# Reordering the first unit's output accumulation and giving the fourth unit its own step plan in a fused attention and mixer kernel

## The chip, the cores and the metric

The kernel runs on one core of a Trainium2 chip. The metric is the device time of one execution, in microseconds (us), and the median of several runs is compared. The core has a matrix engine (TensorE, "PE" in the profile, with "PEld" for its weight loads), a vector engine (VectorE, "DVE"), a scalar engine (ScalarE, "ACT"), GpSimd ("POOL") and SyncE ("SP"), each with its own instruction stream. Transfers between the chip's memory and the on-chip SBUF are issued here by SyncE and GpSimd (two by ScalarE).

## The reference: what is computed

Inputs: q, k, v of shape (8 batches, 8 heads, 576 rows, 64), and four weights. Keys and values are averaged over groups of eight rows, the queries attend to the 72 pooled keys, and the result, with the heads side by side (576 x 512 per batch), goes through an MLP mixer. Its token part mixes the 576 rows through a width of 256; its channel part mixes the 512 channels through a width of 1536.

```python
k_p, v_p = (t.reshape(B, H, S // 8, 8, D).mean(axis=3) for t in (k, v))
scores = (1.0 / np.sqrt(D)) * np.matmul(q, k_p.transpose(0, 1, 3, 2))
attn = softmax(scores)                        # exp(s - max) / (sum + 1e-9)
x = np.matmul(attn, v_p).transpose(0, 2, 1, 3).reshape(B, S, H * D)
h = np.maximum(x.transpose(0, 2, 1) @ w_tok1, 0.0) @ w_tok2
u = x + h.transpose(0, 2, 1)
out = u + np.maximum(u @ w_ch1, 0.0) @ w_ch2  # float32, (8, 576, 512)
```

## The kernel before

**Two halves.** The work of a batch has an attention and token half (`batch_steps`) and a channel half (`unit_steps`). The channel half of batch n is *unit* n; a ninth unit (n = 8) does the 64 rows that each batch leaves over from its four full chunks of 128 rows. While TensorE works on unit n, the attention and token steps of the next batch or of the one after are slipped in between.

**A unit** (lines 438 to 478). First twelve blocks m: four matmuls with `w_ch1` into a one-bank PSUM buffer `p1` (L445), and a relu on ScalarE into `GT` (L449). Then four output chunks c of 128 rows: twelve matmuls over the rows m of `w_ch2` are accumulated in one `p1` buffer (L468); VectorE adds `u` into `o` (L473), and SyncE stores `o` (L476). The pool `ps_one`, from which `p1` comes, has three buffers, taken in turn; each is free again when its reader is done. `w_ch2` is loaded in three pieces of four rows m by `load_ch2` (L138), at the start of the kernel, behind other loads.

**Steps.** `unit_steps` is a generator that yields after every second matmul, 24 times in the blocks and 24 times in the chunks. `unit(n, at)` looks up each yield's number in a plan `at` and emits what stands there, so the order on every engine is written out by hand. In the plans, `<` means batch n, no mark batch n + 1, `>` batch n + 2; a step `lX4` loads q, k or v of batch n + 4. Tail steps (`u4`, `M4`, `T4`) are only done for batches of odd number. Plans `FIRST`, `SECOND` and `THIRD` serve units 0, 1 and 2, and `LATER` all others.

**The steps that matter here:**

- `K0 K1 V0 V1` (L145 to L151): GpSimd sums groups of eight rows of k and v.
- `Q0` to `Q3` (L246): VectorE transposes the queries block by block from the loaded `qb` to `qD`.
- `kpT` (L194): TensorE transposes the pooled keys.
- `s0 s1 s2` (L258, L263): scores on TensorE and the exponential on ScalarE. `s0` needs Q0 and Q1, `s1` needs Q2 and Q3. They use the two two-bank buffers `p2` of the pool `ps_two`.
- `av0` to `av4` (L297; L309 and L315): eight matmuls into a `p2` buffer, then on VectorE a reciprocal `den` and a multiplication into `x` (the tail, av4, into `xt`).
- `at0 at1` (L343) and `u0` to `u4` (L358, L359): the token mixing. The fifth matmul of `at0` reads `xt`.
- `M0 M2 M` (L377, L384): `u` has to be transposed before it can be an operand of the next unit. From unit 3 on this goes through memory: SyncE writes `u` out (`mem`), and four reads bring it back as `v`, with blocks of 32 rows side by side.
- `T0` to `T4` (L390): VectorE transposes the 32 x 32 blocks of `v` into `uT`.
- `lq4 lk4 lv4` (L103, L86): GpSimd issues the loads of batch n + 4. q, k and v have two buffers each, so a load of q waits until the batch two before it has been read by its Q3.

Of the kernel before, what the change touches and what calls it, by code (L numbers as in the profile page):

```python
# [8 lines left out]
FP32 = mybir.dt.float32  # L9
BF16 = mybir.dt.bfloat16  # L10
AF = mybir.ActivationFunctionType
ALU = mybir.AluOpType
# [8 lines left out]
def kernel(  # L21
# [14 lines left out]
    nc = tc.nc  # L36
    B, H, S, D = q.shape
    P = 128
    POOL = 8
    SP = S // POOL  # L40
    BP, BR = 64, S // 64
# [4 lines left out]
    DM = H * D  # L46
    DT = moe_w_tok1.shape[1]
    DC = moe_w_ch1.shape[1]
    NM = DC // P
# [9 lines left out]
    outp = ctx.enter_context(tc.tile_pool(name="outp", bufs=4))  # L59
    ps_one = ctx.enter_context(tc.tile_pool(name="ps_one", bufs=3, space=bass.MemoryType.PSUM))  # L60
# [8 lines left out]
    w_ch2 = singles.tile([P, NM, DM], BF16)  # L69
# [4 lines left out]
    u_tails = singles.tile([P, 4, DM], BF16)  # L74
# [30 lines left out]
    def q_pairs(a0, a1):  # L105
        return q[0, 2 * a0:2 * a1].rearrange("(a l) (p r) d -> (l p) a (r d)", l=2, r=BR)

    def load(key, b):
        if b < B:
            load_q(b) if key == "q" else load_kv(b, k if key == "k" else v, key)  # L110

    def load_tok():
        nc.gpsimd.dma_start(out=f2, in_=moe_w_tok2.rearrange("(c p) n -> p c n", p=P))
        w = moe_w_tok1.rearrange("(p r) n -> p r n", r=BR)
        for half in range(2):
            rows = slice(half * BP, (half + 1) * BP)
            nc.gpsimd.dma_start(out=w_tok1[rows, 0:4, :],
                                in_=w[:, 0:8, :].rearrange("p (c u) n -> p c u n", u=2)[:, :, half])
        for half in range(2):
            rows = slice(half * BP, (half + 1) * BP)  # L120
            nc.gpsimd.dma_start(out=w_tok1[rows, 4 + half, :], in_=w[:, 8, :])

    def permute_tok2():
        src = f2.rearrange("t m (p r) -> t m r p", r=BR)
        dst = w_tok2.rearrange("t m (r p) -> t m r p", p=BP)
        for m in range(2):
            nc.gpsimd.tensor_copy(out=dst[:, m], in_=src[:, m])
        for half in range(2):
            nc.gpsimd.tensor_copy(out=w_tok2t[:, :, half, half * BP:(half + 1) * BP], in_=w_tok2[:, :, 8 * BP:S])

    def load_ch1():
        for g in range(3):
            cols = slice(g * 512, (g + 1) * 512)
            nc.gpsimd.dma_start(out=w_ch1[:, :, cols], in_=moe_w_ch1[:, cols].rearrange("(p c) n -> p c n", c=4))

    def load_ch2(gs):
        for g in gs:
            nc.gpsimd.dma_start(out=w_ch2[:, 4 * g:4 * g + 4, :],  # L138
                                in_=moe_w_ch2[g * 512:(g + 1) * 512, :].rearrange("(c p) n -> p c n", p=P))
# [298 lines left out]
    def unit_steps(n, st):  # L438

        GT = gtp.tile([P, NM, 4 * P], BF16, name="GT")  # L440
        uT = uT_tails if n == B else st["uT"]
        for m in range(NM):
            ps = ps_one.tile([P, 512], FP32, name="p1")
            for kk in range(4):
                nc.tensor.matmul(out=ps, lhsT=w_ch1[:, kk, m * P:(m + 1) * P], rhs=uT[:, kk, :],  # L445
                                 start=(kk == 0), stop=(kk == 3))
                if kk == 1:
                    yield
            nc.scalar.activation(out=GT[:, m, :], in_=ps, func=AF.Relu)  # L449
            yield  # L450
        for c in range(4):
            if n == B and c == 3:
                for a in range(2):
                    cols = slice(a * 256, (a + 1) * 256)
                    ps = ps_one.tile([P, 512], FP32, name="p1")
                    for m in range(NM):
                        nc.tensor.matmul(out=ps[:, 0:256], lhsT=GT[:, m, c * P:(c + 1) * P], rhs=w_ch2[:, m, cols],  # L457
                                         start=(m == 0), stop=(m == NM - 1))
                    o_sb = outp.tile([P, DM], FP32, name="o")[:, 0:256]
                    nc.vector.tensor_tensor(out=o_sb, in0=ps[:, 0:256], in1=(u_tails if n == B else st["u"])[:, c, cols], op=ALU.add)  # L460
                    for half in range(2):
                        (nc.scalar if half else nc.sync).dma_start(
                            out=out[2 * c + half].rearrange("(p r) n -> p r n", r=BR)[:, 8, cols],
                            in_=o_sb[half * BP:(half + 1) * BP, :])
                continue
            ps = ps_one.tile([P, 512], FP32, name="p1")
            for m in range(NM):
                nc.tensor.matmul(out=ps, lhsT=GT[:, m, c * P:(c + 1) * P], rhs=w_ch2[:, m, :],  # L468
                                 start=(m == 0), stop=(m == NM - 1))
                if m % 2 == 1 and m < NM - 1:  # L470
                    yield
            o_sb = outp.tile([P, DM], FP32, name="o")
            nc.vector.tensor_tensor(out=o_sb, in0=ps, in1=(u_tails if n == B else st["u"])[:, c, :], op=ALU.add)  # L473
            for half in range(2):
                b, r = (2 * c + half, 8) if n == B else (n, 2 * c + half)
                nc.sync.dma_start(out=out[b].rearrange("(p r) n -> p r n", r=BR)[:, r, :],  # L476
                                  in_=o_sb[half * BP:(half + 1) * BP, :])
            yield


    HEAD = """c0 c1 d8 q0 d1 q1 d5 kp0 kp1 kt0 d2 o0 e0 kt1 kp2 kp3 o1 e1 kt2 kt3 q2 q3 d2 o2 e2 vpool0 o3 d1 vpool1 e3 d2
# [8 lines left out]
    THIRD = {0: ">K0 >K1 >V0 >V1 s2", 2: "av0", 4: "av1", 6: "av2", 8: "av3", 10: "av4", 12: "at0 >Q0", 13: "at1",  # L490
             15: "u0", 16: "u1", 18: "u2 t0", 19: "u3", 20: "t1 u4", 22: "t2 >Q1", 24: "t3", 26: "t4", 27: ">Q2 >Q3",
             28: ">kpT lq4 lk4 lv4", 29: ">s0", 33: ">s1", 37: ">s2", 39: ">av0", 41: ">av1", 43: ">av2", 45: ">av3", 47: ">av4"}
    LATER = {0: ">K0 >K1 >V0 >V1 at0", 1: "at1", 3: "u4 M4", 4: "u0", 6: "u1 M0", 7: "u2", 9: "u3 M2 M",
             15: ">Q0", 17: ">Q1", 18: ">kpT", 22: ">s0 >Q2", 24: ">Q3 lq4 lk4 lv4", 27: ">s1", 28: "T0", 30: "T1", 31: "T2",
             33: ">s2 T3", 35: "T4", 37: ">av0", 39: ">av1", 41: ">av2", 43: ">av3", 45: ">av4"}
    warm = singles.tile([P, 512], BF16)

    def head(s):
        if s[0] == "d":
            ps = ps_tr.tile([P, 512], FP32, name="pt")  # L500
            for _ in range(int(s[1:])):
                nc.tensor.matmul(out=ps, lhsT=warm[:, 0:P], rhs=warm, start=True, stop=True)
        elif s[0] == "c":
            a = int(s[1:])
            (nc.vector.tensor_copy if a % 2 else nc.scalar.copy)(out=loaded[0, "q"][:, a, 0:BR * D], in_=qf[:, a, :])
        else:
            batches[0][1][s]()

    def unit(n, at):
        if n + 2 < B:  # L510
            batches[n + 2][0]()
        for i, _ in enumerate(unit_steps(n, batches[n][2] if n < B else None)):
            for s in at.get(i, "").split():
                if s[0] == "l":
                    load(s[1], n + int(s[2]))
                    continue
                ahead = {"<": 0, ">": 2}.get(s[0], 1)
                s = s.lstrip("<>")
                if n + ahead < B and ((n + ahead) % 2 or s not in ("u4", "t4", "M4", "T4")):
                    batches[n + ahead][1][s]()  # L520

    with tc.manual_schedule(engines={PE, POOLE, DVE, ACT, SYNC}):
        batches = [batch_steps(b) for b in range(B)]
        nc.vector.memset(warm, 0.0)
        for a in range(2):
            nc.sync.dma_start(out=qf[:, a:a + 1, :], in_=q_pairs(a, a + 1))
        load("k", 0)
        make_identity(nc, ident)
        load("q", 0)
        load("v", 0)  # L530
        nc.vector.memset(kpz, 0.0)
        nc.vector.memset(w_tok1[:, 4:6, :], 0.0)
        nc.vector.memset(w_tok2t, 0.0)
        load_tok()
        load_ch1()
        load("k", 1)
        permute_tok2()
        load("q", 1)
        load("v", 1)
        load_ch2((0, 1, 2))  # L540
        batches[0][0]()
        for s in HEAD.split():
            head(s)
        load("k", 2)
        load("q", 2)
        batches[1][0]()
        unit(0, FIRST)
        unit(1, SECOND)
        unit(2, THIRD)
        for n in range(3, B + 1):  # L550
            unit(n, LATER)


# [28 lines left out]
```

## Time and profile before

| | |
|---|---|
| time, median of 3 runs | 283.78 us (282.54 to 285.27) |
| the profiled execution | 282.39 us, span on the core 280.6 us |
| granted TensorE clock | 1.00 throughout |
| unit 0: blocks, chunks | 24.5 to 39.7, 39.7 to 58.9 us |
| unit 3: blocks, chunks | 122.8 to 138.2, 138.2 to 152.9 us |
| one 512-column matmul, as the profile lists it | 379 ns |
| output add (L473), block transpose (L390), query transpose (L246) | 683, 680, 776 ns |
| load of q, k or v of one batch | 576 KB |

A line of the timeline gives the start and the length in us, the engine, the line of the code, the operation, what is written and read, how many instructions are merged in it, and in brackets how long the engine had been idle before it and what ended that. A line of the waits gives the waiting engine and line, what it waited for, and the sum in us, the number and the longest. The start of a matmul is measured and its end is modelled, so the distance from start to start is the one to work with.

### The profile page before, as it was taken

To read this page: it belongs to the slowest core of one execution; us is meant where nothing else is said; L and a number is where in the kernel's file an instruction comes from. 1 tells how busy PE (TensorE), PEld (TensorE's weight loads), DVE (VectorE), ACT (ScalarE), POOL (GpSimd) and SP (SyncE) were. 2 spreads that over 40 slices of the span, in tenths; PEclk is the share of its full clock that TensorE was granted. 3 is DMA by queue.
4 is the path that set the end of the run, shared out by engine and by line. 5 is a ranking of instruction groups with operands and counts; after the bars stand their busy time and mean duration, and the time that the engine had idled before them with its cause. 6 is when DMAs were issued, how large, how long until landed. Compare 5 with 4: busy or idle time off the path is not lost.

```text
span 280.6 us, 4530 instructions
## 1 busy us (share of the span) xinstructions
PE 271.3 (97%) x1824; PEld 130.9 (47%) x1824; DVE 141.4 (50%) x272; ACT 111.2 (40%) x187; POOL 130.8 (47%) x121
## 2 busy tenths in 40 slices
PE   8999998999999999999997999999999999999994
PEld 3855444444543545454443444544454444444443
DVE  5466975771575757266239454945484152011012
ACT  2543680039405533614830467046703612602600
POOL 8693311999996991998699995000000000000000
PEclk9999999999999999999999999999999999999999
DMA  8999999970199930892796254315232455015014
GB/s 170 184 204 208 204 201 184 229 163 4 21 163 190 234 51 0 141 222 82 156 176 148 56 136 67 80 39 143 46 77 57 122 84 114 0 37 113 2 42 109
DMA packets 36837, 32.68 MB, mean 116 GB/s; under 512 B 14288, under 2 KB 30288, under 8 KB 36816
## 3 DMA queue, kind: packets, MB, share of 16 engines
q0 software_dynamic: 18672, 17.64, 40.0%
q1 hardware_dynamic: 17984, 14.62, 21.1%
q8 instruction: 14, 0.23, 0.3%
q10 hardware_dynamic: 160, 0.13, 0.2%
q14 instruction: 7, 0.06, 0.1%
HBM read 38.21 MB, written 11.80 MB: 178 GB/s over the span
## 4 chain that ended last, share of the span: by engine, by line
PE 73%; DMA 15%; POOL 4%; DVE 3%; ACT 3%; issue 1%; SPq 0%; DVEq 0%; POOLq 0%
PE p L468 29%; PE p L445 25%; DMA w_ch<-in_moe_w_ch_dram 8%; PE p L358 6%; PE p L343 5%; DMA v<-mem 3%; PE p L297 3%; DMA f<-in_moe_w_tok_dram 3%; PE p L258 2%; ACT ex L263 1%; PE pt L368 1%; POOL vr L86 1%; PE p L457 1%; DVE o L473 1%; ACT GT L449 1%
## 5 line engine op out<-in xcount | busy, mean ns | idle before, releaser
L468 PE MATMUL p<-w_ch,GT 128*128 128x512 bf16 x420 | 101.7, 379 | 1.2 <-DMA w_ch<-in_moe_w_ch_dram 1.2
L445 PE MATMUL p<-uT,w_ch 128*128 128x512 bf16 x384 | 94.5, 379 | 0.1
L449 ACT ACTIVATE GT<-p 128x512 bf16<-128x512 f32 x108 | 64.0, 599 | 75.8 <-PE p L445 75.6
L445 PEld LDWEIGHTS <-w_ch 128*128 128x128 bf16 x432 | 40.3, 97 | 48.1 <-issue 4.4
L468 PEld LDWEIGHTS <-GT 128*128 128x128 bf16 x420 | 38.0, 98 | 43.1 <-issue 4.6
L473 DVE TENSOR_TENSOR o<-p,u 128x512 f32<-128x512 f32 x32 | 21.9, 683 | 32.2 <-PE p L468 32.1
L263 ACT ACTIVATE ex<-p 72x1024 bf16<-72x1024 f32 (+1 forms) x42 | 31.7, 807 | 9.1 <-PE p L258 9.1
L146 POOL TENSOR_TENSOR t<-t 72x512 f32<-72x512 f32 x24 | 30.3, 1262 | 1.9
L145 POOL TENSOR_TENSOR t<-kr 72x1024 f32<-72x1024 bf16 x12 | 25.4, 2120 | 9.6 <-DMA kr<-in_k_dram 8.9
L359 DVE TENSOR_TENSOR u<-p,x 128x512 bf16<-128x512 f32 x32 | 22.1, 691 | 13.9 <-PE p L358 13.7
L145 POOL TENSOR_TENSOR t<-vr 72x1024 f32<-72x1024 bf16 x12 | 25.5, 2121 | 0.9
L390 DVE STREAM_TRANSPOSE uT<-v 128x512 bf16<-128x512 bf16 x16 | 10.4, 686 | 27.1 <-DMA v<-mem 27.1
L334 ACT ACTIVATE AT<-p 128x512 bf16<-128x512 f32 x8 | 4.8, 597 | 46.7 <-PE p L343 43.9
L315 DVE TENSOR_TENSOR x<-p,den 128x512 bf16<-128x512 f32 x30 | 20.7, 692 | 1.0
L297 PEld LDWEIGHTS <-ex 72*128 72x128 bf16 x320 | 15.1, 98 | 12.5 <-DVE x L315 3.4
L246 DVE STREAM_TRANSPOSE qD<-qb 128x576 bf16<-128x576 bf16 x28 | 20.3, 791 | 0.0
L297 PE MATMUL p<-vp,ex 72*128 72x65 bf16 x320 | 16.8, 194 | 2.5 <-DVE x L315 2.1
L358 PE MATMUL p<-AT,w_tok 128*128 128x512 bf16 x64 | 19.0, 379 | 0.0
L309 DVE RECIPROCAL den<-p 128x8 f32<-128x8 f32 (+1 forms) x39 | 7.9, 203 | 16.2 <-PE p L297 15.5
L343 PE MATMUL p<-x,w_tok 128*128 128x512 bf16 x56 | 14.4, 380 | 0.0
L336 DVE TENSOR_SCALAR AT<-p 128x512 bf16<-128x512 f32 x8 | 5.5, 692 | 13.4 <-PE p L343 12.6
L258 PE MATMUL p<-qD,kD 32*72 32x512 bf16 (+1 forms) x224 | 12.2, 295 | 0.1
(90 smaller groups left out, 200.4 us busy)
## 6 DMA issues: line engine op xcount, KB each, us to landing
out_dram<-o SPq DMA_DIRECT2D x70, 128.0 KB, 2.4
kr<-in_k_dram POOLq DMA_DIRECT2D x7, 576.0 KB, 11.1
qb<-in_q_dram POOLq DMA_DIRECT2D x7, 576.0 KB, 10.7
vr<-in_v_dram POOLq DMA_DIRECT2D x7, 576.0 KB, 15.0
w_ch<-in_moe_w_ch_dram POOLq DMA_DIRECT2D x6, 512.0 KB, 13.7
mem<-u SPq DMA_DIRECT2D x8, 256.0 KB, 2.1
v<-mem SPq DMA_DIRECT2D x8, 160.0 KB, 3.7
v<-mem SPq DMA_DIRECT2D x8, 128.0 KB, 3.0
```

What stands on the lines that cost most here:

```text
L145: eng.tensor_tensor(out=t4[:, 0:n], in0=t[:, hs, 0:4], in1=t[:, hs, 4:8], op=ALU.add)
L146: eng.tensor_tensor(out=t4[:, 0:n, 0:2], in0=t4[:, 0:n, 0:2], in1=t4[:, 0:n, 2:4], op=ALU.add)
L263: nc.scalar.activation(out=exv[:, a, :, gs.start:gs.stop, n0:n0 + n], in_=pss[a][0:SP, :, 0:len(gs) * n].rearrange("j l (g n) -> j l g n", ...
L297: nc.tensor.matmul(out=halves[h // 4][:, (h % 4) * (D + 1):(h % 4 + 1) * (D + 1)], lhsT=st["ex"][:, h * S + n0:h * S + n0 + P], rhs=st["vp ...
L315: nc.vector.tensor_tensor(out=dst.rearrange("p (a h d) -> p a h d", a=2, d=D), in0=view[:, :, :, 0:D], in1=den[rows, :, :, None].broadcast ...
L343: nc.tensor.matmul(out=ps, lhsT=w_tok1[:, c if c < 4 else 4 + par, m * P:(m + 1) * P], rhs=st["x"][:, c, :] if c < 4 else st["xt"], start= ...
L358: nc.tensor.matmul(out=ps, lhsT=w, rhs=a, start=(i == 0), stop=(i == len(mms) - 1))
L359: nc.vector.tensor_tensor(out=dst, in0=ps, in1=x, op=ALU.add)
L445: nc.tensor.matmul(out=ps, lhsT=w_ch1[:, kk, m * P:(m + 1) * P], rhs=uT[:, kk, :], start=(kk == 0), stop=(kk == 3))
L449: nc.scalar.activation(out=GT[:, m, :], in_=ps, func=AF.Relu)
L468: nc.tensor.matmul(out=ps, lhsT=GT[:, m, c * P:(c + 1) * P], rhs=w_ch2[:, m, :], start=(m == 0), stop=(m == NM - 1))
L473: nc.vector.tensor_tensor(out=o_sb, in0=ps, in1=(u_tails if n == B else st["u"])[:, c, :], op=ALU.add)
```

## The change

Two things are changed.

**Unit 0.** Its output chunks 0 and 1 are interleaved: rows 0 to 7 of chunk 0, rows 0 to 7 of chunk 1, then rows 8 to 11 of each. Rows 8 to 11 are those that read the third piece of `w_ch2`. For this the loop over chunks becomes a list of runs (chunk, first row, end row), and the add and the store become a function called at row 11. For all other units the list gives the order of before, and the last unit's split chunk is moved behind the loop.

**Unit 3.** It gets a plan of its own, `FOURTH`, in which the loads of batch 7 are issued behind T0: the memory reads of `v` are to have the transfer engines to themselves. T0 moves from step 28 to 26; Q2 and Q3 from 22 and 24 to 27; the loads from 24 to 27; s1 from 27 to 32; s2 from 33 to 37; each av by two steps. In `LATER`, the loads are taken out.

```diff
-        for c in range(4):
-            ...
-            ps = ps_one.tile([P, 512], FP32, name="p1")
-            for m in range(NM):
-                nc.tensor.matmul(out=ps, lhsT=GT[:, m, c * P:(c + 1) * P], rhs=w_ch2[:, m, :],
-                                 start=(m == 0), stop=(m == NM - 1))
-                if m % 2 == 1 and m < NM - 1:
-                    yield
+        def store(c, ps):
             o_sb = outp.tile([P, DM], FP32, name="o")
             nc.vector.tensor_tensor(out=o_sb, in0=ps, in1=(u_tails if n == B else st["u"])[:, c, :], op=ALU.add)
             for half in range(2):
                 b, r = (2 * c + half, 8) if n == B else (n, 2 * c + half)
                 nc.sync.dma_start(out=out[b].rearrange("(p r) n -> p r n", r=BR)[:, r, :],
                                   in_=o_sb[half * BP:(half + 1) * BP, :])
-            yield
+
+        runs = [(c, 0, NM) for c in range(3 if n == B else 4)]
+        if n == 0:
+            runs[0:2] = [(c, m, m + w) for m, w in ((0, 8), (8, 4)) for c in range(2)]
+        pss = {}
+        for c, m0, m1 in runs:
+            if m0 == 0:
+                pss[c] = ps_one.tile([P, 512], FP32, name="p1")
+            for m in range(m0, m1):
+                nc.tensor.matmul(out=pss[c], lhsT=GT[:, m, c * P:(c + 1) * P], rhs=w_ch2[:, m, :],
+                                 start=(m == 0), stop=(m == NM - 1))
+                if m == NM - 1:
+                    store(c, pss[c])
+                if m % 2 == 1:
+                    yield
...
+    FOURTH = {0: ">K0 >K1 >V0 >V1 at0", 1: "at1", 3: "u4 M4", 4: "u0", 6: "u1 M0", 7: "u2", 9: "u3 M2 M",
+              15: ">Q0", 17: ">Q1", 18: ">kpT", 22: ">s0", 26: "T0", 27: ">Q2 >Q3 lq4 lk4 lv4", 29: "T1", 31: "T2", 32: ">s1",
+              33: "T3", 35: "T4", 37: ">s2", 39: ">av0", 41: ">av1", 43: ">av2", 45: ">av3", 47: ">av4"}
     LATER = {0: ">K0 >K1 >V0 >V1 at0", 1: "at1", 3: "u4 M4", 4: "u0", 6: "u1 M0", 7: "u2", 9: "u3 M2 M",
-             15: ">Q0", 17: ">Q1", 18: ">kpT", 22: ">s0 >Q2", 24: ">Q3 lq4 lk4 lv4", 27: ">s1", 28: "T0", 30: "T1", 31: "T2",
+             15: ">Q0", 17: ">Q1", 18: ">kpT", 22: ">s0 >Q2", 24: ">Q3", 27: ">s1", 28: "T0", 30: "T1", 31: "T2",
              33: ">s2 T3", 35: "T4", 37: ">av0", 39: ">av1", 41: ">av2", 43: ">av3", 45: ">av4"}
...
         unit(2, THIRD)
-        for n in range(3, B + 1):
+        unit(3, FOURTH)
+        for n in range(4, B + 1):
             unit(n, LATER)
```

More of the change, by code (lines that the diff above doesn't have):

```diff
@@ L450, in unit_steps @@
             yield
-        for c in range(4):
-            if n == B and c == 3:
-                for a in range(2):
-                    cols = slice(a * 256, (a + 1) * 256)
-                    ps = ps_one.tile([P, 512], FP32, name="p1")
-                    for m in range(NM):
-                        nc.tensor.matmul(out=ps[:, 0:256], lhsT=GT[:, m, c * P:(c + 1) * P], rhs=w_ch2[:, m, cols],
-                                         start=(m == 0), stop=(m == NM - 1))
[L459 to L469, printed above, removed]
-                if m % 2 == 1 and m < NM - 1:
-                    yield
+        def store(c, ps):
             o_sb = outp.tile([P, DM], FP32, name="o")
@@ L477, in unit_steps @@
                                   in_=o_sb[half * BP:(half + 1) * BP, :])
-            yield
+        runs = [(c, 0, NM) for c in range(3 if n == B else 4)]
[12 more added lines that the diff above has]
+                    yield
+        if n < B:
+            return
+        for a in range(2):
+            cols = slice(a * 256, (a + 1) * 256)
+            ps = ps_one.tile([P, 512], FP32, name="p1")
+            for m in range(NM):
+                nc.tensor.matmul(out=ps[:, 0:256], lhsT=GT[:, m, 3 * P:4 * P], rhs=w_ch2[:, m, cols],
+                                 start=(m == 0), stop=(m == NM - 1))
+            o_sb = outp.tile([P, DM], FP32, name="o")[:, 0:256]
+            nc.vector.tensor_tensor(out=o_sb, in0=ps[:, 0:256], in1=u_tails[:, 3, cols], op=ALU.add)
+            for half in range(2):
+                (nc.scalar if half else nc.sync).dma_start(
+                    out=out[6 + half].rearrange("(p r) n -> p r n", r=BR)[:, 8, cols],
+                    in_=o_sb[half * BP:(half + 1) * BP, :])
     HEAD = """c0 c1 d8 q0 d1 q1 d5 kp0 kp1 kt0 d2 o0 e0 kt1 kp2 kp3 o1 e1 kt2 kt3 q2 q3 d2 o2 e2 vpool0 o3 d1 vpool1 e3 d2
```

## The prediction

> **What bounds the kernel now.** I read the page's busy table first, then the waits of all engines, then the timeline around the two longest TensorE gaps, and last the same transfer in a quieter unit.
>
> ```profile
> PE 271.3 (97%) x1824; PEld 130.9 (47%) x1824; DVE 141.4 (50%) x272; ACT 111.2 (40%) x187; POOL 130.8 (47%) x121
> ```
>
> TensorE is the bound: 280.6 - 271.3 = 9.3 us of the span are idle, and no other engine is over 50%. The change neither adds nor removes a matmul, so it can only win back idle time. The stage table puts 1.9 us of that in the first 20 us and 3.8 us in the last 30.6 us, stretches with other work; of the remaining 3.6 us, the longest wait of the first line below and the only one of the second hold 3.0:
>
> ```profile
> PE p L297 <- DVE x L315: 2.1, 2, 1.8
> PE p L468 <- DMA w_ch<-in_moe_w_ch_dram: 1.2, 1, 1.2
> ```
>
> The first gap, in unit 0, from the timeline of 36 to 62 us:
>
> ```profile
> 41.61 0.60 PE L468 MATMUL p<-w_ch,GT 128*128 128x512 bf16 x2
> 43.43 0.59 PE L468 MATMUL p<-w_ch,GT 128*128 128x512 bf16 x2 [1.23 <-DMA w_ch<-in_moe_w_ch_dram]
> ```
>
> Row 8 of chunk 0 is the first reader of the third piece of w_ch2. The chain of waits has that piece land at 43.39. Where nothing interrupts, the chain lists 48 of these matmuls in 10.36 us, 0.216 each. So row 8 was due at 41.61 + 2 x 0.216 = 42.04, and the true gap is **1.39 us** (the 1.23 counts from a modelled end).
>
> The second gap, in unit 3, from the timeline of 118 to 153 us:
>
> ```profile
> 134.48 1.92 SPq L384 DMA_DIRECT2D v<-mem  x4
> ...
> 135.34 0.75 POOL L103 DMA_DIRECT2D qb<-in_q_dram  x1 [2.99 <-DVE qD L246]
> 136.09 0.83 POOL L86 DMA_DIRECT2D kr<-in_k_dram  x1
> 136.91 0.80 POOL L86 DMA_DIRECT2D vr<-in_v_dram  x1
> ...
> 144.90 0.71 DVE L390 STREAM_TRANSPOSE uT<-v 128x512 bf16<-128x512 bf16 x1 [9.87 <-DMA v<-mem]
> ...
> 149.46 0.43 PE L297 MATMUL p<-vp,ex 72*128 72x65 bf16 x8 [1.75 <-DVE x L315]
> ```
>
> The small v<-mem reads and batch 7's three loads of 576 KB are issued within 2.5 us of one another. VectorE sits at the first block transpose until 144.90. Behind it stand the output adds, T1 to T3 and the av work (den, x): an av needs the two-bank PSUM buffer that the av two before it used, and av0's x ends only at 149.40. av2 was due when the four matmuls begun at 146.68 had passed, at 147.54; it began at 149.46: **1.92 us**.
>
> The same transfer in unit 5, where there is nothing left to load:
>
> ```profile
> 193.06 2.05 SPq L384 DMA_DIRECT2D v<-mem  x4
> ...
> 197.94 0.71 DVE L390 STREAM_TRANSPOSE uT<-v 128x512 bf16<-128x512 bf16 x1 [4.30 <-DMA v<-mem]
> ```
>
> From first issue to transpose: 4.88 us there, 5.57 in unit 4 and 5.60 in unit 6 (pieces of 160 KB instead of 128), but 10.42 in unit 3, whose pieces are 128 KB.
>
> [...] L468 is listed at 379 ns but starts every 216, and o, den and x all stand behind the waiting L390. So I take gaps between starts, and I ask what is queued behind each wait. [...]
>
> **The change, part by part** (times on the profile-before's clock unless said).
>
> *Unit 0.* Order before: c0 rows 0-11, then c1. Order after: c0 rows 0-7, c1 rows 0-7, c0 rows 8-11, c1 rows 8-11. No instruction is added, and the steps at which av1 to av4 and at0 stand keep their numbers. After c0's row 7 (42.04) come eight rows of c1 (1.73 us), av2 and av3 (0.26 each, from the starts 43.86 and 44.12): row 8 of c0 comes at 44.29, 0.9 us after the piece landed. The wait of 1.39 is gone with 0.9 to spare. What it might cost: two accumulations are open at once in a ring of three one-bank buffers. at0 takes the third; at1 takes c0's after c0's add, and c2 takes c1's. c0's last row ends at 45.41, but VectorE first finishes av4's xt at about 46.1, then c0's add (0.68) at 46.8; at1 is due at 47.35. c1's last row ends at 47.35 and its add at about 48.25; at1's five matmuls (1.08) hold TensorE until 48.43. Both fit, the second by 0.2 us; it stood in the same relation before (add at 48.95 to 49.64, c2 at 49.99). Cost 0 to 0.2; I take 0. Sum: **-1.39**.
>
> *Does the shift last?* Up to 130 us no wait of TensorE on a transfer remains, so what follows moves along unless a GpSimd pool is late: batch 2's k pool ends at 56.49 and is read at 60.01, its last v pool would end at 65.0 (60.92 + 2.12 + 1.26 + 0.73) and is read at 68.69. Both are over 3 us early. Nothing is lost.
>
> *Unit 3.* [...] L103 of the loads already waits for Q3 (the 2.99 above), because it overwrites the buffer that Q3 reads; with Q3 behind T0, the loads can start only after v has landed. Then v takes what it takes in unit 5: 134.48 + 4.88 = 139.36. T0 (0.71), Q2 and Q3 (2.84 for four at 132.19, 0.71 each) end at 141.49. Who waits: s1, at step 32. s0 ends at 137.78, two L445 follow, then c0's twelve rows and six of c1 from 138.22: s1 is due at 138.22 + 18 x 0.216 = 142.11. It finds Q3 done with **0.6 us** to spare; at the slower 5.60 of unit 6 it would wait 0.1. c0's add, T1 and T2 follow by 143.7, T3 by 144.4, c1's add by about 145.1; av0 comes at about 146.4 and finds VectorE free. The 1.92 us are gone.
>
> New cost: av4 stands at step 47 in place of 45, directly ahead of unit 4's at0. Unit 2 shows what this makes:
>
> ```profile
> 123.24 1.03 PE L343 MATMUL p<-x,w_tok 128*128 128x512 bf16 x4
> ...
> 123.58 0.68 DVE L315 TENSOR_TENSOR xt<-p,den 64x512 bf16<-64x512 f32 x1
> ...
> 124.31 0.38 PE L343 MATMUL p<-xt,w_tok 128*128 128x512 bf16 x1
> ```
>
> The fifth matmul was due at 123.24 + 4 x 0.216 = 124.10: it lost 0.21. In unit 3 before, it came on time (153.30, then 154.16). Sum for unit 3: -1.92 + 0.21 = **-1.71**.
>
> *The delayed loads.* GpSimd issues them after 141.5 in place of 135.3, and batch 6's pools, queued behind, start at about 143.9 in place of 137.7. With 8.2 us for the k half and 17.4 in all they end at 152 and 161; kpT of batch 6 is at 165.98, its av later still. The last load took 13.9 us to land, so it lands near 157; batch 7's pools cannot start before 161, and batch 5's v<-mem in unit 4 is issued at 165.29. All hidden: 0. Taking these loads out of the later plan removes nothing: from unit 4 on there is no batch left for them.
>
> Total: -1.39 - 1.92 + 0.21 = -3.10. From the median: 283.78 - 3.10 = **280.7 us** (-1.1%).
>
> **The rivals.**
> A. The forecast, 280.7 (280.0 to 281.6 with the small bounds above): chance 0.58.
> B. More than that. The profiled execution was one of 282.39, 1.4 under the median, and still lost 3.3 us in these two gaps. If the others are longer because these same landings come later, slack now swallows it and the median falls to 282.39 - 3.10 = 279.3. For it: both gaps end on a transfer. Against: no trace of a longer execution. 0.17.
> C. Half of it. In unit 3 the gain is eaten by something not in my list (s1, s2 and the av follow more tightly, a spill or store behind the loads is late), and only unit 0 pays: 283.78 - 1.39 = 282.4. For it: only 0.6 us of slack at s1. 0.17.
> D. Slower. The v reads are late for a reason other than the loads, and land at 144.90 as before; then T0, Q2, Q3 end at 147.03, s1 waits 4.92 on TensorE, and 280.7 + 4.9 = 285.6. For it: the change puts TensorE's own work behind this landing. Against: units 4 to 6. 0.08.
>
> **How the numbers follow.** Likeliest is A, 280.7. B and C are nearly as likely as one another and a median of a few runs wanders (282.54 to 285.27 before), so the range reaches from just under B to past C, short of D: 279.0 to 283.0. Faster by over 1% means under 280.94: about six tenths of A (0.35) and B (0.17), 0.52. Within 1%: the rest of A, C and most of D, 0.43. Slower by over 1% (286.6) needs D with a further wait: 0.05.
>
> **What would show it.** In unit 0: the wait of L468 on w_ch gone, no new wait of L343 or L468 on L473. In unit 3: L390's first start some 5 us after the first L384 instead of 10.4, L103 after it, PE L297's wait of 1.75 gone, no wait of L258 on L246. At unit 4's start: 0.2 us ahead of the fifth L343. Wrong if s1 waits for qD, if v still needs 8 us or more, or if kpT of batch 6 waits for GpSimd.

## The result, and the profile after

| | before | after |
|---|---|---|
| median of 6 executions | 284.99 us (282.54 to 289.55) | 280.11 us (279.35 to 281.21) |
| ratio after / before, 95% interval | | 0.985 (0.980 to 0.990) |
| span of the profiled execution | 280.6 us | 278.3 us |

The changed kernel is 1.5% faster, 280.11 us against a forecast of 280.7. Two differences stand side by side here and don't agree: the medians lie 4.9 us apart, the two traces 2.3 us. And the scatter has shrunk, from 7 us to under 2. (The ratio leaves out the longest executions, so it shows a little less than the medians.) Where that comes from is the subject of the experiments.

The waits of TensorE after, from 40 us to the end (waiting line, what it waited for, sum in us, number, longest):

```profile
PE p L445 <- issue: 0.3, 2, 0.2
PE p L467 <- issue: 0.3, 2, 0.2
PE p L297 <- ACT ex L263: 0.2, 1, 0.2
PE p L343 <- DVE xt L315: 0.2, 1, 0.2
```

L467 is the output matmul (L468 before). Both waits of before are gone: no matmul of an output chunk waits for `w_ch`, no av for an `x`. In their place stands one small wait of `at0` for `xt`.

The timeline of unit 0 after:

```profile
42.30 1.03 PE L467 MATMUL p<-w_ch,GT 128*128 128x512 bf16 x4
...
44.28 0.42 PE L297 MATMUL p<-vp,ex 72*128 72x65 bf16 x8
44.55 0.81 PE L467 MATMUL p<-w_ch,GT 128*128 128x512 bf16 x3
```

Chunk 0's row 8 is the third matmul of the last line, at 44.98, and nothing interrupts the pace. (One record of the four is missing: the av behind it begins on time, at 45.41.) But the chunks began at 40.41 in this execution and at 39.73 in the one before.

The timeline of unit 3 after:

```profile
133.77 1.92 SPq L384 DMA_DIRECT2D v<-mem  x4
...
139.15 0.71 DVE L390 STREAM_TRANSPOSE uT<-v 128x512 bf16<-128x512 bf16 x1 [6.18 <-DMA v<-mem]
139.78 1.46 DVE L246 STREAM_TRANSPOSE qD<-qb 128x576 bf16<-128x576 bf16 x2
...
141.49 0.63 PE L258 MATMUL p<-qD,kD 32*72 32x512 bf16 x8
141.56 0.75 POOL L103 DMA_DIRECT2D qb<-in_q_dram  x1 [9.90 <-DVE qD L246]
...
150.86 0.81 PE L343 MATMUL p<-x,w_tok 128*128 128x512 bf16 x3
151.87 0.38 PE L343 MATMUL p<-xt,w_tok 128*128 128x512 bf16 x1 [0.20 <-DVE xt L315]
```

The load of q (L103) is now issued behind Q3, 7.8 us after the first read of `v` instead of 0.9; `v` lands 5.38 us after its first issue instead of 10.42; s1 (L258) finds Q3 done at 141.24. From the first row of unit 3's chunk 0 to the fifth matmul of unit 4's `at0` it is 151.87 - 137.51 = 14.36 us, against 154.16 - 138.22 = 15.94 before.

The two traces thus differ by +0.68 up to unit 0's chunks (a part that was not changed), -1.38 in these chunks (17.85 us to unit 1's first matmul against 19.23), and -1.58 in unit 3: together -2.28, the 2.3 us of the spans.

### The profile page after: what moved, and what is told of

The parts are those of the page before. It is cut to its first block, busy times and chain, and to the rows that moved or that the text cites. A ratio compares the mean times of both kernels' runs of the same rounds, so it can differ in the third digit from the quotient of the medians.

```text
span 278.3 us, 4495 instructions
## 1 busy us (share of the span) xinstructions
PE 268.9 (97%) x1790; PEld 130.9 (47%) x1824; DVE 141.8 (51%) x272; ACT 111.2 (40%) x187; POOL 130.8 (47%) x121
## 4 chain that ended last, share of the span: by engine, by line
PE 83%; DMA 8%; ACT 3%; DVE 2%; POOL 2%; issue 1%; POOLq 0%
PE p L467 32%; PE p L445 30%; PE p L358 6%; PE p L343 5%; DMA kr<-in_k_dram 5%; PE p L258 4%; PE p L297 3%; DMA f<-in_moe_w_tok_dram 3%; ACT ex L263 1%; PE pt L368 1%; PE p L479 1%; ACT GT L449 1%; DVE o L453 1%; POOL vr L86 1%; POOL kr L86 1%
## 5 line engine op out<-in xcount | busy, mean ns | idle before, releaser
L467 PE MATMUL p<-w_ch,GT 128*128 128x512 bf16 x404 | 99.2, 379 | 1.0 <-issue 0.3
L445 PE MATMUL p<-uT,w_ch 128*128 128x512 bf16 x373 | 92.7, 379 | 1.1 <-issue 0.3
L467 PEld LDWEIGHTS <-GT 128*128 128x128 bf16 x420 | 38.0, 98 | 41.9 <-issue 3.1
L390 DVE STREAM_TRANSPOSE uT<-v 128x512 bf16<-128x512 bf16 x16 | 10.4, 686 | 23.7 <-DMA v<-mem 23.7
L297 PEld LDWEIGHTS <-ex 72*128 72x128 bf16 x320 | 15.3, 98 | 10.4 <-DVE x L315 0.8
L297 PE MATMUL p<-vp,ex 72*128 72x65 bf16 x320 | 16.8, 194 | 1.0 <-DVE x L315 0.6
L103 POOL DMA_DIRECT2D qb<-in_q_dram x7 | 5.1, 730 | 21.5 <-DVE qD L246 20.3
```

The source lines that it names most:

```text
L297: nc.tensor.matmul(out=halves[h // 4][:, (h % 4) * (D + 1):(h % 4 + 1) * (D + 1)], lhsT=st["ex"][:, h * S + n0:h * S + n0 + P], rhs=st["vp ...
L467: nc.tensor.matmul(out=pss[c], lhsT=GT[:, m, c * P:(c + 1) * P], rhs=w_ch2[:, m, :], start=(m == 0), stop=(m == NM - 1))
```

## Experiments

My theory after the result: each part removes the gap of TensorE that it is aimed at, and the gap of unit 3 is longer in many executions than in the one profiled before, because `v` lands later in them. Rivals: the scatter belongs to unit 0's landing of `w_ch2`; or it is the moved steps that pay, and not the held-back loads.

### Each part alone

`e1`: unit 0's interleave only.

```diff
-        unit(3, FOURTH)
-        for n in range(4, B + 1):
+        for n in range(3, B + 1):
             unit(n, LATER)     # LATER with "24: >Q3 lq4 lk4 lv4" as before
```

> Only the interleave of unit 0; unit 3 follows the plan LATER as before, with the loads of batch 7 at step 24. If the two parts add up as worked out: the wait of row 8 on the third piece of w_ch2 (gap 1.39 us) gone, unit 3 unchanged with its transfer v<-mem at some 10 us and TensorE's gap of 1.9 us; 1.4 us faster than before (ratio 0.995). If the wide scatter of the executions before comes from unit 3, this kernel scatters as widely as before; if it comes from the landing of w_ch2, it scatters as little as the changed kernel.

`e2`: unit 3's plan only.

```diff
-        if n == 0:
-            runs[0:2] = [(c, m, m + w) for m, w in ((0, 8), (8, 4)) for c in range(2)]
```

> Only the plan of unit 3; unit 0 goes through chunk 0 and then chunk 1 as before. If the two parts add up: gap at row 8 still about 1.4 us, gap at av2 of unit 3 gone, 0.2 to 0.4 us lost at unit 4's fifth matmul of at0; 1.5 to 1.7 us faster than before in a like execution (ratio 0.994 to 0.995). Rival, that unit 3 is worth more in a typical execution than in the one profiled before: 3 us or more faster (ratio 0.990 or less) and as little scatter as the changed kernel.

Measured: unit 0 alone 285.52 us (281.52 to 290.02), ratio 1.005 (0.999 to 1.010); unit 3 alone 279.82 us (279.52 to 281.71), ratio 0.985 (0.980 to 0.990); the kernel before, on the same chip, 284.80 (281.28 to 291.18). All of the measured gain, and the whole of the narrower scatter, come from unit 3's plan. The interleave alone gives nothing that can be measured, and not the 1.4 us of my sum. Where the scatter is small the answer is the same: with unit 3's plan and without the interleave the median is 279.82 us, with both (`e4` below, the same session, av one step earlier) 280.08.

Why it gives nothing is read from unit 0's chunks in all six traces that lack the interleave and load `w_ch2` as before. The length runs from the chunks' first matmul to unit 1's first; without any gap it is 17.85:

| kernel | chunks begin | length | gap |
|---|---|---|---|
| before, the trace of the prediction | 39.73 | 19.23 | 1.38 |
| before, equal program `e3` | 40.55 | 18.15 | 0.30 |
| before, `e9` | 40.25 | 18.02 | 0.17 |
| before, `e10` | 40.61 | 18.06 | 0.21 |
| unit 3 alone, `e2` | 42.05 | 17.85 | 0 |
| before without batch 7's loads, `e5` | 41.09 | 17.85 | 0 |

The piece's landing moves little: the chain has it at 43.39, 43.13 and 43.10 in the first, second and fourth row, and in `e9` row 8, the third matmul of this line, was due at 42.57 and lost 0.17:

```profile
42.14 1.19 PE L468 MATMUL p<-w_ch,GT 128*128 128x512 bf16 x4
```

So the landings lie within some 0.7 us, and the starts of the chunks within 2.3. The trace that I predicted from had the earliest start of the six and so the longest wait. A kernel that reaches the chunks sooner waits longer for the same landing. With the interleave an early start is kept: in `e6` below the chunks began at 39.54 and took 17.86 us.

### The place of the loads in the plan

`e3`: the loads are written behind T0, nothing else is moved.

```diff
-             ... 24: ">Q3 lq4 lk4 lv4", 27: ">s1", 28: "T0", 30: "T1", ...
+             ... 24: ">Q3", 27: ">s1", 28: "T0 lq4 lk4 lv4", 30: "T1", ...
```

> The kernel before with the three loads of batch 7 written behind T0 in the plan (step 28 in place of 24), and no other step moved. GpSimd's order of instructions stays what it was, and the load of q waits for Q3, which is still ahead of T0 on VectorE. My theory: nothing changes, loads issued at about 135 us, v<-mem some 10 us, ratio 1.00. Rival, that the place of the loads in the plan is what counts: 1.9 us faster (0.993). It also shows how far two equal programs lie apart.

Measured: 285.04 us, ratio 1.002 (0.997 to 1.006): no change. Every engine has the instructions of before in the order of before; L103 was issued at 135.10, held by Q3 alone. What holds the loads in the changed kernel is Q3's new place behind T0 on VectorE.

The execution that was traced here took 290.12 us. It is the kernel before in one of its long executions:

```profile
134.24 2.96 SPq L384 DMA_DIRECT2D v<-mem  x4
...
135.10 0.75 POOL L103 DMA_DIRECT2D qb<-in_q_dram  x1 [2.99 <-DVE qD L246]
...
150.35 0.71 DVE L390 STREAM_TRANSPOSE uT<-v 128x512 bf16<-128x512 bf16 x1 [15.57 <-DMA v<-mem]
...
154.91 0.62 PE L297 MATMUL p<-vp,ex 72*128 72x65 bf16 x8 [7.46 <-DVE x L315]
155.34 1.90 PE L468 MATMUL p<-w_ch,GT 128*128 128x512 bf16 x4
```

SyncE's second read took 1.50 us to issue instead of 0.48, so only the first of the four reads was issued in full before GpSimd's first load, instead of two; the last landed 13.53 us after its issue, against 8.85 in the trace of the prediction. That the one led to the other is likely, but not shown. av2 was due at 147.50, so TensorE stood for 7.41 us. And the four matmuls behind the gap take 1.90 us instead of 1.03. The stages of this trace show why (the number behind the engines' busy times is the granted TensorE clock):

```profile
145.00:150.00 5.00, 2.39 (x24) 1.20 (x23) 0.00 (x0) 0.00 (x0) 4.69 (x5) 0.96 0.79 126
150.00:155.00 5.00, 0.09 (x2) 0.09 (x3) 4.58 (x9) 0.00 (x0) 4.69 (x5) 0.50 0.28 60
155.00:160.00 5.00, 5.00 (x34) 2.60 (x35) 3.13 (x7) 0.00 (x0) 4.77 (x4) 0.51 0.50 108
```

By its mean in stretches of 1 us (0.82 in 149 to 150, 0.50 up to 159, 0.56 in 159 to 160) the clock is halved from 149.64 to 159.88 us, that is for the end of the gap and the 5 us behind it, which costs some 2.5 us more (an estimate: half of the 5). Gap longer by 5.5 us (7.41 against 1.92) and 2.5 us of half clock are 8.0; the span is longer by 288.3 - 280.6 = 7.7. This one trace pays for the late landing of `v` twice.

### The loads taken away

`e5`: the kernel before without the loads of batch 7 (batch 7 computes on batch 5's q, k and v).

```diff
-        if b < B:
+        if b == B - 1:
+            loaded[b, key] = loaded[b - 2, key]
+        elif b < B:
             load_q(b) if key == "q" else load_kv(b, k if key == "k" else v, key)
```

> The kernel before, every step where it was, but without the three loads of batch 7 in unit 3: batch 7 works on the q, k and v of batch 5, so its outputs are those of batch 5's attention. If it is the loads that hold up v<-mem: the transfer takes about 5 us from its first issue, TensorE's gap at av2 is gone without any step moved, the executions scatter as little as those of the changed kernel, and the median is 4.5 to 5.5 us under the kernel before. Rival, that the order of the steps on VectorE makes the difference (Q2 and Q3 behind T0, later av): v<-mem still takes 8 us or more, and the median stays within 1.5 us of before.

Measured: 280.09 us (279.02 to 281.12), ratio 0.986 (0.981 to 0.990), against a median of 284.43 before on the same chip. Its unit 3 (the code's lines stand two lower: L386 is L384, L392 is L390, L299 is L297):

```profile
134.47 1.92 SPq L386 DMA_DIRECT2D v<-mem  x4
...
140.04 0.71 DVE L392 STREAM_TRANSPOSE uT<-v 128x512 bf16<-128x512 bf16 x1 [5.01 <-DMA v<-mem]
...
146.67 1.03 PE L470 MATMUL p<-w_ch,GT 128*128 128x512 bf16 x4
147.53 0.42 PE L299 MATMUL p<-vp,ex 72*128 72x65 bf16 x8
```

With no step moved, `v` lands in 5.57 us, av2 comes on time at 147.53, and time and scatter are those of the changed kernel; the median is 4.3 us under the kernel before, just short of the 4.5 expected. The loads are the cause, and the order of the steps is only the means to hold them back. (Whether it is their transfers or their issue on GpSimd that slows the reads, this run doesn't separate.) This kernel also bounds the gain: holding the loads back is worth as much as not having them.

### The loads not held, in the new plan

`e6`: k and v are loaded ahead of q; only q waits for Q3.

```diff
-    FOURTH = {... 27: ">Q2 >Q3 lq4 lk4 lv4", ...
+    FOURTH = {... 27: ">Q2 >Q3 lk4 lv4 lq4", ...
```

> The changed kernel, but GpSimd issues batch 7's loads in the order k, v, q in place of q, k, v. Only q's load waits for Q3; those of k and v can start as soon as GpSimd is done with batch 5's pools, some 3 us ahead of the v<-mem reads. If holding the loads back is what pays: v<-mem takes 8 us or more again, TensorE now waits at s1 for Q2 and Q3 behind T0 (3 to 8 us), the scatter is back, and the time is that of before or longer (283 to 290). [...] Rival, that the later places of s1, s2 and av alone absorb a late landing: under 281.

Measured: 288.62 us (287.95 to 289.13), ratio 1.016 (1.011 to 1.020): 8.5 us over the changed kernel, from the order of three lines in the plan.

```profile
130.76 0.84 POOL L86 DMA_DIRECT2D kr<-in_k_dram  x1
131.59 0.80 POOL L86 DMA_DIRECT2D vr<-in_v_dram  x1
132.97 4.97 SPq L384 DMA_DIRECT2D v<-mem  x4
...
145.31 0.71 DVE L390 STREAM_TRANSPOSE uT<-v 128x512 bf16<-128x512 bf16 x1 [13.18 <-DMA v<-mem]
...
146.78 1.32 PE L258 MATMUL p<-qD,kD 32*72 32x512 bf16 x8 [6.06 <-DVE qD L246]
```

`v` needs 12.3 us, T0 keeps Q2 and Q3 behind it, and s1, due at 136.67 + 18 x 0.216 = 140.56, starts at 146.78: 6.2 us. This is the prediction's case D, made on purpose, and the later places of s1 and av don't absorb it. One point of the expectation fell: the scatter didn't come back. A likely reason, not tested: here the loads of k and v are issued 2.2 and 1.4 us ahead of the reads, while in the kernel before the two start within a microsecond of each other (134.48 and 135.34 in the trace of the prediction, 134.24 and 135.10 in `e3`), and how they fall out differs between those two executions: the last read landed after 8.85 and 13.53 us.

### What the halved clock costs

`e8`: the kernel of `e6`, with 16 matmuls put ahead of s1 whose result nobody reads (`unit` also gets three lines that pass such a step on to `head`).

```diff
-              ... 32: ">s1",
+              ... 32: "d16 >s1",      # d16: 16 matmuls of 512 columns on a buffer of zeros
```

> The kernel whose k and v loads are not held (gap of 6.1 us at s1, clock at 0.50 behind it), with 16 matmuls of 512 columns put ahead of s1 that nothing reads: 3.5 us of additional work for TensorE, all inside the gap, whose idle rest is then 2.7 us. If the halved clock follows from the length of the idle stretch: the clock stays at 1.00 behind the gap, and the kernel with more work is 2 to 3 us faster than without (about 286). Rival, that the clock falls for another reason, or that the dummy work delays s1: the same time as without, or longer (288.6 or more).

The stages 145 to 150 and 150 to 155 us, first of `e6`, then of `e8`:

```profile
145.00:150.00 5.00, 3.20 (x13) 1.06 (x14) 4.43 (x7) 1.88 (x2) 2.29 (x2) 0.50 0.17 10
150.00:155.00 5.00, 5.00 (x48) 2.33 (x47) 1.90 (x4) 0.70 (x3) 4.69 (x5) 0.82 0.92 215
```

```profile
145.00:150.00 5.00, 1.99 (x15) 0.66 (x13) 3.25 (x6) 0.67 (x1) 0.85 (x2) 1.00 0.05 12
150.00:155.00 5.00, 4.84 (x55) 2.52 (x54) 3.60 (x8) 1.92 (x4) 4.76 (x4) 1.00 0.93 163
```

With the idle stretch cut to 2.9 us the clock stays at 1.00 in this execution, although `v` takes as long (12.5 us). From the first row of chunk 0 to av0, `e8` needs 152.63 - 137.97 = 14.66 us and `e6` 153.29 - 136.67 = 16.62: 2.0 us less with 3.5 us more of TensorE work. s1 begins equally late in both, 10.25 and 10.11 us after that row, so the 2 us are won behind the gap. That speaks for the idle stretch as the cause of the halved clock, and puts its cost here at 2 us. But it is one execution: the other three of `e8` have a mean clock of 0.992 or 0.993 (`e6`: 0.986 or 0.987), so the filling did not keep the full clock every time; how long they stood idle was not traced. As a whole the kernel took 288.07 us, ratio 1.023 (1.016 to 1.030); it ran in another session than `e6`, where the kernel before took 282.0, so that the totals don't bear out the 2 us. Only the stretch does.

The gaps seen, and the clock behind them: 1.92 us (before) 1.00; 2.91 (`e8`) 1.00; 3.32 (`e7a` below) 1.00; 3.12 (`e11` below) 0.50; 6.22 (`e6`) 0.50; 7.41 (`e3`) 0.50. Read from the mean clocks of the stages, the halved stretches last some 3.4 us in `e11` (0.88, 0.50 and 0.77 in 45 to 47, 47 to 49 and 49 to 51 us), 6.8 in `e6` (0.50 and 0.82 above) and 10.2 in `e3`, about once, twice and three times the same. They begin some 3.2 us after TensorE's next matmul was due in `e11`, 4.4 in `e6` and 2.1 in `e3` (149.64 against 147.50). So no single length parts these traces: one gap of 3.32 us passed at 1.00, and in `e3` the clock was down after 2.1. What decides between the two is not shown.

### The kernel before, twice more

> The kernel before once more, for a further trace of unit 3. Theory: its time follows the landing of the last piece of v<-mem; a landing some 9 us after issue goes with 281 to 283 us, one of 13 us or more with 288 to 291 and a halved clock; in between, a gap of 3 to 5 us and 284 to 287.

> As the run ahead of it: the kernel before, one more trace. Same theory: the longer the last piece of v<-mem takes, the longer the gap at av2 and the whole[...].

Measured: 281.99 and 281.94 us. The last piece of `v` landed 9.16 and 8.71 us after its issue, and the waits of av2 were these:

```profile
149.07 0.43 PE L297 MATMUL p<-vp,ex 72*128 72x65 bf16 x8 [2.06 <-DVE x L315]
```

```profile
149.02 0.43 PE L297 MATMUL p<-vp,ex 72*128 72x65 bf16 x8 [1.60 <-DVE x L315]
```

From the due times (147.07 and 147.47) the gaps are 2.00 and 1.55 us. With the trace of the prediction (8.85 us, 282.39) and that of `e3` (13.53 us, 290.12) these are four traces of one program, three short and one long, as expected. (The trace of `e1`, whose unit 3 is that of before, is a fourth short one: 8.6 us, a gap of 1.42, 281.52.)

None of the executions of 284 to 287 us, where the median lies, was traced. But the mean granted clock of every execution was recorded, and it parts them in two. Of the 53 executions of the kernel before that were timed beside the experiments, 18 have a mean clock of 0.997 or more and take 280.66 to 283.95 us (median 281.7); 35 have 0.994 or less and take 283.00 to 291.18 (median 284.9). One stretch of 3.4 us at half clock, the length seen in `e11` below, makes a mean of 0.994 over 283 us, by estimate (1 - 0.5 x 3.4 / 283). So the typical execution of the kernel before has at least one such stretch, and the three short traces of it, with a mean clock of 1.00, are all of the quicker third. All 24 executions of the changed kernel, `e2`, `e4` and `e5` have 0.997 or more. That the gap behind which the clock falls is the one in unit 3 follows from `e2` and `e5`, which change only unit 3's plan or the loads in it; how long it is in these executions is not shown.

### What the interleave is worth when the piece is late

`e7a`: unit 3's plan without the interleave, the third piece of `w_ch2` issued behind batch 2's k. `e7b`: the same in the full changed kernel.

```diff
-        load_ch2((0, 1, 2))
+        load_ch2((0, 1))
...
         load("k", 2)
+        load_ch2((2,))
```

> Unit 3's new plan with unit 0 as before, and the third piece of w_ch2 issued behind batch 2's load of k (576 KB) in place of ahead of it, so that it lands some 2.8 us later. Chunk 0 meets it at row 8: a gap of about 3 us there (0.3 us in the trace of the equal program of before), some 2.5 us slower than unit 3's plan alone: 282 to 283.

> The same late third piece in the full changed kernel, whose interleave meets it 2.0 to 2.3 us later. If the interleave is worth what the order of the rows says: a gap of about 1 us or less, and 2.0 us faster than the kernel with the late piece and no interleave; about 281. Rival, that TensorE's pace in unit 0 is set by something else, so that the interleave is worth nothing even then: both alike.

Measured: 285.25 us without the interleave (282.26 to 287.46), 280.75 with it (279.85 to 281.82). The gap at chunk 0's row 8, without and with it:

```profile
46.70 0.59 PE L465 MATMUL p<-w_ch,GT 128*128 128x512 bf16 x2 [3.16 <-DMA w_ch<-in_moe_w_ch_dram]
```

```profile
46.72 0.59 PE L467 MATMUL p<-w_ch,GT 128*128 128x512 bf16 x2 [1.53 <-DMA w_ch<-in_moe_w_ch_dram]
```

The landing is the same; the interleaved kernel meets it later. From the first row of the chunks to unit 1's first matmul it is 21.16 us without and 19.54 with the interleave (59.99 - 40.45). The rival falls: the interleave works as worked out, when there is something to wait for. But the medians differ by 4.5 us and not by the 2 us expected, and the kernel without it is 5.4 us over its like without the late piece (`e2`, 279.82), where I had expected 2.5. One more trace of it:

> The late third piece without the interleave, one more trace: its median was 5.4 us over the kernel without the late piece, and its one trace shows only 3.3 us of gap at row 8 and a full clock. If the rest is the clock, an execution of 285 us or more shows a gap over 3.3 us in unit 0 and a clock of 0.5 behind it; rival, that the rest lies elsewhere: a full clock and a second wait.

Measured: 285.46 us, with this at row 8 and behind it:

```profile
46.49 1.01 PE L465 MATMUL p<-w_ch,GT 128*128 128x512 bf16 x2 [2.96 <-DMA w_ch<-in_moe_w_ch_dram]
...
47.76 1.90 PE L465 MATMUL p<-w_ch,GT 128*128 128x512 bf16 x4
```

The gap is no longer than in the first trace (3.12 us from the due time, against 3.32), but the clock fell to 0.50 for some 3.4 us. The chunks took 63.63 - 41.05 = 22.58 us, 1.4 more than in the first trace. So my expectation that the gap had to exceed 3.3 us was wrong, and that the clock makes a good part of the missing 2.9 us was right: 10 of the 14 executions of `e7a` have a mean clock of 0.994 or less, none of the six of `e7b`. In this trace, close to the median, the chunks take 4.7 us more than 17.85; the 0.7 us left of the 5.4 I can't place (the two medians come from different sessions).

### A version without the new wait

`e4`: the changed kernel with its five av one step earlier.

```diff
-    FOURTH = {... 39: ">av0", 41: ">av1", 43: ">av2", 45: ">av3", 47: ">av4"}
+    FOURTH = {... 38: ">av0", 40: ">av1", 42: ">av2", 44: ">av3", 46: ">av4"}
```

> The changed kernel with the five av of unit 3's plan one step earlier (38, 40, 42, 44, 46). Theory: the wait of the fifth matmul of at0 in unit 4 for xt, 0.37 us in the profile after, goes away, since two matmuls and an output add then stand between; s2 at 37 leaves av0 its buffer just in time. 0.3 to 0.4 us faster than the changed kernel. Rival: the gap moves to av0, which then waits up to 0.4 us for the exponential of s2, and the time stays that of the changed kernel.

Measured: 280.08 us, ratio 0.986 (0.981 to 0.990), the same as the changed kernel.

```profile
150.84 1.03 PE L343 MATMUL p<-x,w_tok 128*128 128x512 bf16 x4
...
151.70 0.38 PE L343 MATMUL p<-xt,w_tok 128*128 128x512 bf16 x1
```

The fifth matmul comes on time. From chunk 0's first row it is 151.70 - 137.60 = 14.10 us instead of 14.36; av0 comes 0.11 late, so a part of the 0.37 moves there, as the rival had it. A gain of 0.26 in the trace is too small for these medians to tell.

## Why the prediction was right, and where it was not

The time, the direction and the mechanism of unit 3 were right; two terms of the sum were off, in opposite directions, and the total of -3.10 came as near to the measured gain (4.9 us in the medians, 1.5% in the ratio) as it did only because they partly cancelled. That the time itself came within 0.6 us is luck besides: I subtracted from 283.78, the median of three executions of before, and the median of six was 284.99.

- **Unit 0, -1.39: mis-sized.** The mechanism is as written (the wait is gone, row 8 has time to spare, c2 and at1 wait for nothing), and the gap in that trace was 1.38. But I took one execution's gap for the typical one. In three further traces of before it is 0.17 to 0.30, since the chunks begin 0.5 to 0.9 us later there and the piece does not. Alone the interleave measures at a ratio of 1.005 (0.999 to 1.010).
- **Unit 3, -1.92: right for that execution, too small for the typical one.** The gap was removed, by what was said: the loads behind Q3, Q3 behind T0, `v` landing in about 5 us (5.38; I had taken 4.88). `e2` gains 5.0 us in the median, `e5` 4.3. In a long execution the gap is 7.41 us, and I had no term for the half clock seen with such a gap (0.50 for 10.2 us in `e3`); two thirds of the executions of before (35 of 53) have a mean clock that fits such a stretch.
- **s1's slack: 0.6 us forecast, about 0.2 measured** (Q3 done at 141.24, s1 due at 141.40), as `v` took 0.5 us longer. It sufficed here. In the trace of `e2`, where `v` took 5.56, s1 began 0.1 us late, the forecast's own figure for 5.60. `e6` shows what hangs on it.
- **The new wait at `at0`, +0.21: it was 0.37.** The fifth matmul was due at 150.21 + 6 x 0.216 = 151.51 and came at 151.87. `e4` removes it.
- **The delayed loads, 0: right.** Counted from the first read of `v`, since the two traces are 0.7 us apart there, L103 came at 7.8 us (forecast 7.0) and batch 6's pools at 10.2 (9.4), and there is no wait of TensorE on GpSimd in the table after.
- **Rival B was half right.** Longer executions do lose more, on a landing, and the median fell by 4.9 us; but on that of `v`, not of both. I had given it less weight than the sum of the terms because there was no trace of a longer execution. The scatter of 282.54 to 285.27 in the times before was the evidence I had.

## What to carry to other kernels

A gap that ends on a transfer had no one size here: in four traces of the kernel before it was 0.17 to 1.38 us in unit 0 and 1.55 to 7.41 in unit 3. Before pricing its removal, compare the traced execution with the median, and ask which transfers are issued beside it and whether their order is fixed (`v` took 10.42 us beside batch 7's loads, 5.57 without them in `e5`). To keep one transfer clear of another, make the second's issue depend on an instruction that comes after the first has landed: with Q3 behind T0, L103 was issued at 141.56, after T0 at 139.15. Moving its line in the program was not enough: in `e3` it was issued at 135.10. And a gap of TensorE can cost more than its length: with gaps of 3.12, 6.22 and 7.41 us the clock was at 0.50 for 3.4, 6.8 and 10.2 us, in part or wholly behind the gap, and in the longest it was down after 2.1 us. With gaps of 1.4 to 2.0 us, and with one of 2.91 and one of 3.32, it stayed at 1.00.

## What the runs showed that I had not expected

Two equal starts of the same two transfers, 0.9 us apart, let the last piece of the small one land 8.7 to 9.2 us after issue in three traces and 13.5 us in a fourth, with 1.50 us instead of 0.48 for issuing one of its pieces. With a gap of 3.12 us the TensorE clock was at 0.50 for 3.4 us in one trace, and with one of 3.32 us it stayed at 1.00 in another of the same program. And 3.5 us of matmuls that nobody reads, put into a gap, made the stretch around it 2.0 us shorter in the execution traced.
